# Turning the K cache with VectorE block transpositions instead of TensorE transposes in a decode step (adaLN, cached sliding-window attention, squared-ReLU MLP)

## The chip, the cores and the metric

The kernel runs on one core of a Trainium2 chip. The metric is device time of one execution in microseconds (us), lower is better. A core has TensorE (PE in the profile), VectorE (DVE), ScalarE (ACT), GpSimd (POOL) and SyncE (SP, here the engine that issues the large loads), each with its own queue that it works off in order, and 16 DMA engines that move data between HBM and the core's SBUF. Matrix products land in PSUM, eight banks of 128 partitions x 512 fp32 values. All data here is fp32.

## What is computed

One decode step for 8 sequences: a conditioning vector `c` gives six modulation vectors; then layer norm, attention over the last 2048 cached positions with 32 query heads on 8 key/value heads of width 128, layer norm again, and an MLP with squared ReLU.

```python
mod = (_silu(c) @ w_mod).reshape(c.shape[0], 6, 1, -1)          # (8,512) @ (512,3072)
h = _layernorm(x) * (1 + ca) + sa
# attention: Hq=32, Hkv=8, Dh=128, Sk=8192, W=2048
q = (h @ wq)                                                    # (512,4096)
k, v = k_cache[:, :, Sk - W:, :], v_cache[:, :, Sk - W:, :]     # each used by 4 query heads
p = softmax(q @ k.T * Dh ** -0.5)
x = x + ga * ((p @ v) @ wo)                                     # (4096,512)
h = _layernorm(x) * (1 + cb) + sb
x = x + gb * (relu(h @ w1 + b1) ** 2 @ w2 + b2)                 # F = 1792
```

The windows of K and V are 67.1 MB each; the weights are some 30.5 MB more. Every byte is used once.

## The kernel before, in words

**Loads.** All large loads go out from SyncE's queue, in the order of the list `loads` (lines 143 to 153), into fixed slots in SBUF: two "big" slots of 4.19 MB (32 KB per partition) and five "small" ones of 2.10 MB. `pump()` issues the next load of the list as soon as a slot of its size is free, and `done()` frees a slot where its last reader has been issued; the load then waits on the chip for that reader. The list is strict: a load that waits for its slot holds up all that stand behind it. It begins with K block 0, four modulation weights, four q weights, K block 1, V block 0, K block 2; after that K and V blocks and pieces of `wo` alternate, and the last entries are V block 31, the biases, `tail` (the last part of `wo` and half of `w1`, a big slot), the rest of `w1` (a small slot) and `w2` (a big slot).

**K and V blocks.** A K block `q` (16 of them) holds four sequences of one key/value head: partition `4p + u` holds 64 consecutive positions of sequence `u`. Block `2 hk` has sequences 0 to 3 of head `hk`, block `2 hk + 1` sequences 4 to 7. A V block `n` (32 of them) holds two sequences of one head.

**Turning K.** A score product needs K with the 128 values of a key along the partitions. `transposes(q, g, e)` (line 223) does an eighth of a block: eight PE transposes of 128x128 (line 232) into PSUM, two banks of them in the pool `ps_kt`, and two copies of 128x512 out of PSUM into the tile `kT` (line 234), one by ACT and one by DVE. The tile pool `ktp` has three `kT` buffers, each for one `(q, g)`. After the last eighth of a block, `done(("K", q))` frees its slot (line 237).

**Scores.** `scores(q, g)` (line 346) makes four products, one per sequence `u`, of 32 columns of q times 512 keys. The 32 columns are a sliding window over a tile of zeros with the four query heads in the middle (`qwin`, line 186, filled by `window`, line 343, out of `qall`), so the four heads land on other rows for each `(g, c)` and all eight `(g, c)` of one head add up in one PSUM bank `s_ps`: 128 rows (sequence `u`, key group `g`, half `c`, query head) by 512 keys.

**Softmax.** `soft_a` copies the scores to SBUF (ACT) and takes row maxima (DVE). `soft_b` turns the maxima into a row with PE and shares the maximum among the rows of one query head. `soft_c` brings it back to a column, and ACT's exponential writes `pr`, every fourth element, so that DVE can double it (line 410). `soft_d` turns `pr` with eight PE transposes (line 426) and DVE multiplies them out of PSUM with a mask `mine` (line 429), which keeps for each partition the half of the sequences that it holds.

**Weighted sum.** `weighted(n, h)` (line 441) multiplies the turned probabilities with a V block in two halves; behind the second half DVE adds up the diagonal blocks into `o_sb` (lines 464 and 466). `gather` and `project_o` bring the head's result through `wo` into `wo_ps`.

**Order.** The schedule is written out by hand: the loop at line 502 has 37 steps `s`; each of the first 32 turns half a K block (four calls of `transposes`) and makes two groups of scores, and V runs five steps behind (`PV_LAG`). Each engine works in the order of the calls. Ahead of the loop, the four parts of K block 0 (`EARLY`, line 263) are turned between the modulation products, and the fourth in step 0. `turn_q(0)` and `turn_q(1)` (line 328) turn the two halves of q, the second in step 1. Step 2 is the first that works on K block 1. Behind the loop come the output projection, the second layer norm and the MLP, with a few products that only keep PE busy (`spin`).

Of the kernel before, what the change touches and what calls it, by code (L numbers as in the profile page):

```python
# [20 lines left out]
def tile_adaln_cached_attention_mlp(  # L21
# [34 lines left out]
    ktp = ctx.enter_context(tc.tile_pool(name="ktp", bufs=3))  # L56
    ps_kt = ctx.enter_context(tc.tile_pool(name="ps_kt", bufs=2, space=bass.MemoryType.PSUM))
# [140 lines left out]
    u4 = consts.tile([P, 4], F32, name="u4")  # L198
    nc.vector.tensor_reduce(u4, ident.rearrange("p (u x) -> p u x", u=4), axis=AX.X, op=ALU.add)
    for c in range(2):  # L200
        nc.vector.tensor_scalar(bq[:, 4 * c : 4 * c + 4], u4, uq[:, c : c + 1], None, op0=ALU.mult)
# [11 lines left out]

    mine = consts.tile([P, 2, REP], F32, name="mine")
    odd = ident.rearrange("p (r u) -> p u r", u=2)
    for u in range(2):
        nc.vector.tensor_reduce(mine[:, u, 0:1], odd[:, u, :], axis=AX.X, op=ALU.add)
        for t in range(1, REP):
            nc.vector.tensor_copy(mine[:, u, t : t + 1], mine[:, u, 0:1])

    KTS = {}

    def transposes(q, g, e):

        k = slot(("K", q), DH)
        if e == 0:
            KTS[q, g] = ktp.tile([P, 4, 16, 32], F32, name="kT")
        t = KTS[q, g]
        for a in range(2):
            p = ps_kt.tile([P, 4, P], F32, name="kt_ps")  # L230
            for i in range(4):
                nc.tensor.transpose(p[:, i, :], k[:, 32 * e + 16 * a + 4 * g + i, :], ident)  # L232
            i = 8 * e + 4 * a
            (nc.vector.tensor_copy if a else nc.scalar.copy)(  # L234
                t[:, :, i : i + 4, :], p.rearrange("p i (r u) -> p u i r", u=4)
            )
        if g == 3 and e == 1:
            done(("K", q))
# [24 lines left out]
    EARLY = [(0, g) for g in range(4)]  # L263
# [23 lines left out]
    for kc in range(NQ):  # L287
        if kc < 3:
            transposes(0, kc, 0)
            transposes(0, kc, 1)  # L290
        wv = slot(("mod", kc), 6 * D)[:, 0].rearrange("p (m q n) -> p m q n", m=6, q=NQ)
        for pm, m0, m1 in zip(pms, (0, 4), (4, 6)):
            for q in range(NQ):
                nc.tensor.matmul(  # L294
                    pm[32 * q : 32 * q + 32, : (m1 - m0) * P].rearrange("p (m n) -> p m n", n=P),
                    cT[:, kc, :],
                    wv[:, m0:m1, q, :],
                    start=(kc == 0),
                    stop=(kc == NQ - 1),
                )  # L300
        done(("mod", kc))
# [26 lines left out]
    def turn_q(r):  # L328
        qs = work.tile([P, 512], F32, name="qs", tag="a", bufs=1)
        nc.scalar.copy(qs, pqs[r])  # L330
        pT_ = ps_m.tile([P, 512], F32, name="m_ps", tag="m_ps")
        for t in range(REP):
            nc.tensor.transpose(pT_[:, t * P : (t + 1) * P], qs[:, t * P : (t + 1) * P], ident)  # L333
        nc.vector.tensor_copy(  # L334
            qall[:, 4 * r : 4 * r + 4].rearrange("p g b t -> p t g b"),
            pT_.rearrange("p (t g b) -> p t g b", t=REP, g=4)[:, :, :, :B],
        )
# [4 lines left out]
    P_, PT_, RZ_, RZP_, OS_, O_, MX_, SS_ = {}, {}, {}, {}, {}, {}, {}, {}  # L342
    def window(hk):
        nc.vector.tensor_copy(qwin[hk % 2][:, :, 28:32], qall[:, hk])  # L344

    def scores(q, g):

        hk, c = divmod(q, 2)
        if c == 0 and g == 0:
            s_ps[0] = ps_1.tile([P, 512], F32, name="s_ps")  # L350
            if hk == 0:
                window(0)
        if c == 1 and g == 0 and hk + 1 < HKV:
            window(hk + 1)
        o = 28 - 4 * (2 * g + c)
        kT = KTS.pop((q, g))
        for u in range(4):
            nc.tensor.matmul(  # L358
                s_ps[0][32 * u : 32 * u + 32, :],
                qwin[hk % 2][:, 4 * c + u, o : o + 32],  # L360
                kT[:, u].rearrange("p i r -> p (i r)"),
                start=(c == 0 and g == 0),
                stop=(c == 1 and g == 3),
            )
# [8 lines left out]
    def soft_b(hk):  # L373
        pm = ps_m.tile([P, 512], F32, name="m_ps", tag="m_ps")
# [5 lines left out]
            pm[0:1, :P].rearrange("p (u g r) -> p u r g", u=4, g=4),  # L380
# [3 lines left out]
        nc.vector.tensor_scalar(  # L384
            mrow.rearrange("p u (g r) -> p u g r", g=4),
            m1.rearrange("p (u r) -> p u r", u=4)[:, :, None, :].to_broadcast([1, 4, 4, 8]),
            -SCALE,
            None,
            op0=ALU.mult,
        )  # L390
        MX_[hk] = mrow

    def soft_c(hk):
# [6 lines left out]
        pr = work.tile([P, 8, H, 2], F32, name="pr", bufs=1)  # L400
        z = work.tile([P, 1], F32, name="z")
        nc.scalar.activation(  # L402
            pr.rearrange("p i (r e) u -> p e i r u", e=2)[:, :, :, :, 0],
            SS_.pop(hk).rearrange("p (e i r) -> p e i r", e=2, i=8),
            AF.Exp,
            bias=nm,
            scale=SCALE,
            accum_out=z,
        )
        nc.vector.tensor_copy(pr[:, :, :, 1], pr[:, :, :, 0])  # L410
        zs = work.tile([P, B], F32, name="zs")
        nc.vector.tensor_scalar(zs, bq, z, None, op0=ALU.mult)  # L412
        P_[hk], RZP_[hk] = pr, zs
# [5 lines left out]
    def soft_d(hk):  # L419

        pr = P_.pop(hk)
        PT_[hk] = work.tile([P, 2, 4 * C, 4, 2 * REP], F32, name="pT", bufs=1)
        for a in range(2):
            pp = ps_m.tile([P, 512], F32, name="m_ps", tag="m_ps")
            for i in range(4):
                nc.tensor.transpose(  # L426
                    pp[:, i * P : (i + 1) * P], pr[:, 4 * a + i].rearrange("p r u -> p (r u)"), ident
                )
            nc.vector.tensor_mul(  # L429
                PT_[hk][:, a].rearrange("p x i r -> p i x r"),  # L430
                pp.rearrange("p (i x r) -> p i x r", i=4, r=2 * REP),
                mine.rearrange("p u t -> p (u t)")[:, None, None, :].to_broadcast([P, 4, 4 * C, 2 * REP]),
            )
# [7 lines left out]
    def weighted(n, h):  # L441
# [6 lines left out]
        for g in range(4):  # L448
            j = 16 * h + 4 * g
            nc.tensor.matmul(  # L450
                o[32 * g : 32 * g + 32].rearrange("p j d -> p (j d)"),
                PT_[hk][:, h, 4 * c + g].rearrange("p i r -> p (i r)"),
                v[:, j : j + 4, :].rearrange("p j d -> p (j d)"),
                start=(h == 0),
                stop=(h == 1),
            )
# [44 lines left out]

    for s in range(N + PV_LAG + 1):
# [27 lines left out]
        if s == 0:  # L530
            transposes(0, 3, 0)
            transposes(0, 3, 1)
# [13 lines left out]
    spin_ps = ps_kt.tile([P, 4, P], F32, name="kt_ps")  # L546
# [117 lines left out]
```

## Time and profile before

| what | value |
|---|---|
| median of 3 runs | 397.34 us (397.11 to 398.51) |
| the profiled execution | 397.39 us |
| its span, first to last instruction | 395.6 us |
| DMA traffic in the span | 165.22 MB, mean 418 GB/s |
| ACT busy | 97.5 us |
| mean granted PE clock | 0.974 |

The span is what the trace covers; the profiled execution's own time is the span and a little before and after it. Busy time of an engine counts computing instructions only. In the lists of groups a row is: line, engine, operation, output<-input by the program's names, shapes, count, then busy time in us and mean ns of one, then the idle time of the engine just before these instructions and what ended it.

### The profile page before, as it was taken

Reading aid. Unit: us, or ns where it says so; the run is one execution under the profiler, and the core shown is the slowest. Engines: PE = TensorE matmul, PEld = TensorE weight load, DVE = VectorE, ACT = ScalarE, POOL = GpSimd, SP = SyncE. Lnnn points to the kernel's source line nnn. Section 1 sums busy time; section 2 is a strip of 40 time slices with the busy share of each in tenths; the row PEclk is TensorE's granted clock in tenths of the full one; section 3 lists DMA queues with packets and bytes.
Section 4 is the critical chain, followed back from the end, with each engine's and each line's share of the span. In section 5 each row is a group of like instructions: output and inputs, shape, how many; then the busy total and the mean of one; then the engine's idle time right before and its main releaser. Section 6 shows DMA issues by size and latency. Waiting matters only on the chain.

```text
span 395.6 us, 5981 instructions
## 1 busy us (share of the span) xinstructions
PE 330.5 (84%) x2550; PEld 162.4 (41%) x2550; DVE 178.2 (45%) x416; ACT 97.5 (25%) x169; POOL 2.4 (1%) x12
## 2 busy tenths in 40 slices
PE   0683489979998697999889988998859998997696
PEld 0440035554454353444444544444534454432133
DVE  6121023454456353655464556454524455455531
ACT  2220022342232122322332222222211241222010
POOL 2000000000000000000000000000000000000000
PEclk9996889999999998999999999999999999999999
DMA  8999999999999999999999999999999999999993
GB/s 335 410 430 427 441 418 442 417 419 446 404 435 442 414 432 422 441 417 451 403 449 409 444 416 434 434 419 421 437 419 447 417 437 413 431 431 421 422 424 136
DMA packets 10363, 165.22 MB, mean 418 GB/s; under 512 B 1112, under 2 KB 1376, under 8 KB 1632
## 3 DMA queue, kind: packets, MB, share of 16 engines
q1 hardware_dynamic: 10192, 164.71, 97.9%
q8 instruction: 20, 0.33, 0.3%
q10 hardware_dynamic: 144, 0.13, 0.1%
q14 instruction: 7, 0.06, 0.0%
HBM read 164.77 MB, written 0.07 MB: 417 GB/s over the span
## 4 chain that ended last, share of the span: by engine, by line
DMA 46%; PE 42%; DVE 7%; ACT 4%; issue 1%; ACTq 0%; DVEq 0%
DMA big<-in_A_k_cache_dram 31%; PE kt_ps L232 20%; PE s_ps L358 9%; PE o_ps L450 7%; DMA small<-in_A_wq_dram 6%; DMA big<-in_B_w_dram 5%; DMA small<-in_A_v_cache_dram 4%; ACT pr L402 2%; DVE o_sb L466 2%; DVE kT L234 2%; PE m_ps L294 1%; ACT kT L234 1%; DVE pT L429 1%; PE m_ps L319 1%; DVE pr L410 1%
## 5 line engine op out<-in xcount | busy, mean ns | idle before, releaser
L232 PE MATMUL kt_ps<-ident,big 128*128 128x128 f32 x1024 | 145.5, 285 | 22.6 <-DMA big<-in_A_k_cache_dram 18.3
L232 PEld LDWEIGHTS kt_ps<-ident,big 128*128 128x128 f32 x1024 | 112.8, 144 | 111.9 <-ACT kT L234 68.1
L234 DVE COPY kT<-kt_ps 128x512 f32<-128x512 f32 x128 | 88.2, 689 | 121.5 <-PE kt_ps L232 121.5
L234 ACT COPY kT<-kt_ps 128x512 f32<-128x512 f32 x128 | 75.0, 586 | 209.4 <-PE kt_ps L232 208.6
L358 PE MATMUL s_ps<-kT,qwin 128*32 128x512 f32 x512 | 69.2, 614 | 0.8 <-DVE qwin L344 0.8
L450 PE MATMUL o_ps<-small,pT 128*32 128x512 f32 x512 | 67.1, 602 | 1.9 <-DMA small<-in_A_v_cache_dram 1.9
L466 DVE SCALAR_TENSOR_TENSOR o_sb<-o_ps,diag,o_sb 128x128 f32<-128x128 f32 x96 | 33.7, 351 | 3.4
L319 PE MATMUL m_ps<-small,h1T 128*32 128x512 f32 x64 | 11.5, 857 | 11.5 <-DMA small<-in_A_wq_dram 11.5
L450 PEld LDWEIGHTS o_ps<-small,pT 128*32 128x32 f32 x512 | 11.7, 108 | 22.7 <-issue 22.7
L464 DVE TENSOR_SCALAR o_sb<-o_ps,diag 128x128 f32<-128x128 f32 x32 | 11.2, 350 | 16.3 <-PE o_ps L450 15.6
L358 PEld LDWEIGHTS s_ps<-kT,qwin 128*32 128x32 f32 x512 | 10.3, 109 | 12.8 <-issue 11.1
L402 ACT ACTIVATE pr<-ss,nm 128x512 f32<-128x512 f32 x8 | 9.9, 1244 | 11.8 <-DVE nm L399 11.7
L334 DVE COPY qall<-m_ps 128x128 f32<-128x128 f32 x2 | 0.8, 390 | 23.0 <-PE m_ps L333 23.0
L435 PE MATMUL m_ps<-zs,tsel 128*128 128x8 f32 x16 | 3.1, 266 | 8.7 <-DVE pT L429 8.7
L319 PEld LDWEIGHTS m_ps<-small,h1T 128*32 128x32 f32 x64 | 2.1, 134 | 19.8 <-DMA small<-in_A_wq_dram 10.6
L429 DVE TENSOR_TENSOR pT<-m_ps,mine 128x512 f32<-128x512 f32 x16 | 10.2, 680 | 0.0
L474 PE MATMUL m_ps<-o_sb,pick 128*128 128x512 f32 x16 | 8.4, 606 | 1.8 <-DVE o_sb L466 1.6
L426 PEld LDWEIGHTS m_ps<-ident,pr 128*128 128x128 f32 x64 | 6.9, 141 | 7.0 <-issue 7.0
L426 PE MATMUL m_ps<-ident,pr 128*128 128x128 f32 x64 | 8.7, 278 | 1.1 <-DVE zs L412 1.1
L370 DVE TENSOR_REDUCE mx<-ss 128x1 f32<-128x512 f32 x8 | 5.5, 688 | 8.6 <-ACT ss L368 8.6
L410 DVE COPY pr<-pr 128x512 f32<-128x512 f32 x8 | 3.4, 430 | 12.3 <-ACT pr L402 12.3
L294 PE MATMUL m_ps<-small,cT 128*32 128x512 f32 (+1 forms) x64 | 6.6, 531 | 1.3 <-DMA small<-in_w_mod_dram 1.3
(123 smaller groups left out, 105.4 us busy)
## 6 DMA issues: line engine op xcount, KB each, us to landing
big<-in_A_k_cache_dram SPq DMA_DIRECT2D x16, 4096.0 KB, 21.9
small<-in_A_v_cache_dram SPq DMA_DIRECT2D x32, 2048.0 KB, 23.2
small<-in_A_wq_dram SPq DMA_DIRECT2D x4, 2048.0 KB, 21.8
small<-in_w_mod_dram SPq DMA_DIRECT2D x4, 1536.0 KB, 17.4
small<-in_A_wo_dram SPq DMA_DIRECT2D x3, 2048.0 KB, 19.9
big<-in_A_wo_dram SPq DMA_DIRECT2D x2, 1024.0 KB, 17.8
big<-in_B_w_dram SPq DMA_DIRECT2D x1, 2048.0 KB, 23.4
big<-in_B_w_dram SPq DMA_DIRECT2D x1, 1792.0 KB, 22.0
```

The lines of the kernel that those rows point to most:

```text
L232: nc.tensor.transpose(p[:, i, :], k[:, 32 * e + 16 * a + 4 * g + i, :], ident)
L234: (nc.vector.tensor_copy if a else nc.scalar.copy)(t[:, :, i : i + 4, :], p.rearrange("p i (r u) -> p u i r", u=4))
L294: nc.tensor.matmul(pm[32 * q : 32 * q + 32, : (m1 - m0) * P].rearrange("p (m n) -> p m n", n=P), cT[:, kc, :], wv[:, m0:m1, q, :], start=( ...
L319: nc.tensor.matmul(pqs[r][32 * g : 32 * g + 32, :], hT[:, kc, :], w[:, 4 * r + g, :], start=(kc == 0), stop=(kc == NQ - 1),)
L358: nc.tensor.matmul(s_ps[0][32 * u : 32 * u + 32, :], qwin[hk % 2][:, 4 * c + u, o : o + 32], kT[:, u].rearrange("p i r -> p (i r)"), start ...
L402: nc.scalar.activation(pr.rearrange("p i (r e) u -> p e i r u", e=2)[:, :, :, :, 0], SS_.pop(hk).rearrange("p (e i r) -> p e i r", e=2, i= ...
L426: nc.tensor.transpose(pp[:, i * P : (i + 1) * P], pr[:, 4 * a + i].rearrange("p r u -> p (r u)"), ident)
L429: nc.vector.tensor_mul(PT_[hk][:, a].rearrange("p x i r -> p i x r"), pp.rearrange("p (i x r) -> p i x r", i=4, r=2 * REP), mine.rearrange ...
L450: nc.tensor.matmul(o[32 * g : 32 * g + 32].rearrange("p j d -> p (j d)"), PT_[hk][:, h, 4 * c + g].rearrange("p i r -> p (i r)"), v[:, j : ...
L464: nc.vector.tensor_scalar(d, o[:, 0, :], diag[:, 0:1], None, op0=ALU.mult)
L466: nc.vector.scalar_tensor_tensor(d, o[:, j, :], diag[:, j : j + 1], d, op0=ALU.mult, op1=ALU.add)
L474: nc.tensor.matmul(pp, pick.rearrange("p t u -> p (t u)"), o.rearrange("p c d -> p (c d)"), start=True, stop=True)
```

## The change

K is turned by DVE's transposition, which turns each 32x32 square of a tile by itself, directly from SBUF to SBUF. One call of `transposes(q, j, e)` is now a single DVE instruction on 32 of a block's 64 positions and on 32 of the 128 values. A square of 32 partitions holds eight groups `p` of four sequences `u`; behind the transposition partition `32 i + x` holds value `32 j + x` of the keys that lay on partitions `32 i` to `32 i + 31`. So a `kT` tile holds one quarter `j` of the values for all keys of the block, and on its partitions lie four different key groups `i`. The score product must take quarter `j` of q on each of the four partition groups, and put the result of group `i` on rows of its own: `qst` holds q in such pieces with zeros between them. They are made per head by a product with `sel` that repeats a quarter `j` of q on all four partition groups (`window`), out of `qbd`, which holds q block by block between zeros; four ACT and four DVE copies put them in place.

The score rows then stand in another order (sequence, key group, half, query head); `soft_b` multiplies the copied scores with a permutation matrix `perm`, and the exponential reads the result out of PSUM and writes `pr` contiguously. `pr2` takes the place of the doubling and of the mask: DVE and ACT write one half each, multiplied with 0 or 1. One DVE transposition of 128x1024 takes the place of eight PE transposes and two masked copies in `soft_d`.

The pool `ps_kt` is gone (its two banks go to the products of `window` and `soft_b`), there are two `kT` buffers in place of three, and only two of the four parts of K block 0 are turned ahead of the loop; the other two are turned in step 1 by the loop itself.

```diff
-    ktp = ctx.enter_context(tc.tile_pool(name="ktp", bufs=3))
-    ps_kt = ctx.enter_context(tc.tile_pool(name="ps_kt", bufs=2, space=bass.MemoryType.PSUM))
+    ktp = ctx.enter_context(tc.tile_pool(name="ktp", bufs=2))
...
-    qall = consts.tile([P, HKV, B, REP], F32, name="qall")
-    qwin = [consts.tile([P, B, 60], F32, name=f"qwin{i}") for i in range(2)]
-    for t in qwin:
+    qbd = consts.tile([P, HKV, 4, B * REP], F32, name="qbd")
+    qst = [consts.tile([P, B, 4, 4, 2, REP], F32, name=f"qst{i}") for i in range(2)]
+    for t in [qbd, *qst]:
         nc.gpsimd.memset(t, 0.0)
...
+    perm = consts.tile([P, P], F32, name="perm")
+    nc.vector.tensor_copy(
+        perm.rearrange("r (i u w) -> r i u w", i=4, u=4), ident.rearrange("r (u i w) -> r i u w", i=4, u=4)
+    )
...
-    def transposes(q, g, e):
+    def transposes(q, j, e):
         k = slot(("K", q), DH)
         if e == 0:
-            KTS[q, g] = ktp.tile([P, 4, 16, 32], F32, name="kT")
-        t = KTS[q, g]
-        for a in range(2):
-            p = ps_kt.tile([P, 4, P], F32, name="kt_ps")
-            for i in range(4):
-                nc.tensor.transpose(p[:, i, :], k[:, 32 * e + 16 * a + 4 * g + i, :], ident)
-            i = 8 * e + 4 * a
-            (nc.vector.tensor_copy if a else nc.scalar.copy)(
-                t[:, :, i : i + 4, :], p.rearrange("p i (r u) -> p u i r", u=4)
-            )
-        if g == 3 and e == 1:
+            KTS[q, j] = ktp.tile([P, 4, 64, 8], F32, name="kT")
+        rows = slice(32 * e, 32 * e + 32)
+        nc.vector.transpose(
+            KTS[q, j][:, :, rows].rearrange("q u r p -> q r p u"),
+            k[:, rows, 32 * j : 32 * j + 32].rearrange("q r (p u) -> q r p u", u=4),
+        )
+        if j == 3 and e == 1:
             done(("K", q))
...
-    EARLY = [(0, g) for g in range(4)]
+    EARLY = [(0, 0), (0, 1)]
...
-        if kc < 3:
+        if kc < 2:
             transposes(0, kc, 0)
             transposes(0, kc, 1)
...
-        nc.vector.tensor_copy(
-            qall[:, 4 * r : 4 * r + 4].rearrange("p g b t -> p t g b"),
-            pT_.rearrange("p (t g b) -> p t g b", t=REP, g=4)[:, :, :, :B],
-        )
+        for j in range(4):
+            b = slice(32 * j, 32 * j + 32)
+            nc.vector.tensor_copy(
+                qbd[b, 4 * r : 4 * r + 4, j].rearrange("p g (b t) -> p t g b", t=REP),
+                pT_[b].rearrange("p (t g b) -> p t g b", t=REP, g=4)[:, :, :, :B],
+            )
...
     def window(hk):
-        nc.vector.tensor_copy(qwin[hk % 2][:, :, 28:32], qall[:, hk])
+        pq = ps_1.tile([P, 512], F32, name="q_ps")
+        nc.tensor.matmul(pq[:, :P], sel, qbd[:, hk].rearrange("p j x -> p (j x)"), start=True, stop=True)
+        pv = pq[:, :P].rearrange("p (j c u t) -> p c u j t", j=4, c=2, u=4)
+        for i in range(4):
+            b = slice(32 * i, 32 * i + 32)
+            for c in range(2):
+                (nc.vector.tensor_copy if c else nc.scalar.copy)(
+                    qst[hk % 2][b, 4 * c : 4 * c + 4, :, i, c], pv[b, c]
+                )
...
-                qwin[hk % 2][:, 4 * c + u, o : o + 32],
-                kT[:, u].rearrange("p i r -> p (i r)"),
+                qst[hk % 2][:, 4 * c + u, j].rearrange("p i c t -> p (i c t)"),
+                kT[:, u].rearrange("q r p -> q (r p)"),
...
     def soft_b(hk):
+        sp = ps_1.tile([P, 512], F32, name="p_ps")
+        nc.tensor.matmul(sp, perm, SS_.pop(hk), start=True, stop=True)
+        SS_[hk] = sp
...
     def soft_c(hk):
...
-        nc.vector.tensor_copy(pr[:, :, :, 1], pr[:, :, :, 0])
+        X_[hk] = work.tile([P, 32, 8, 2, 2], F32, name="pr2", bufs=1)
+        for c in range(2):
+            o, i = X_[hk][:, :, :, :, c], pr.rearrange("p e j x -> p j x e")
+            if c:
+                nc.scalar.mul(o, i, uq[:, c : c + 1])
+            else:
+                nc.vector.tensor_scalar(o, i, uq[:, c : c + 1], None, op0=ALU.mult)
...
     def soft_d(hk):
-        for a in range(2):
-            pp = ps_m.tile([P, 512], F32, name="m_ps", tag="m_ps")
-            for i in range(4):
-                nc.tensor.transpose(
-                    pp[:, i * P : (i + 1) * P], pr[:, 4 * a + i].rearrange("p r u -> p (r u)"), ident
-                )
-            nc.vector.tensor_mul(
...
+        PT_[hk] = work.tile([P, 4, 32, 2 * REP], F32, name="pT", bufs=1)
+        nc.vector.transpose(
+            PT_[hk].rearrange("p u j r -> p j u r"),
+            X_.pop(hk).rearrange("p j (u r) e c -> p j u (r e c)", u=4),
+        )
...
-        if s == 0:
-            transposes(0, 3, 0)
-            transposes(0, 3, 1)
```

More of the change, by code (lines that the diff above doesn't have):

```diff
@@ L383, in soft_b @@
         )
[L384 to L389, printed above, removed]
-        )
+        nc.vector.tensor_scalar(mrow, m1[:, None, :].to_broadcast([1, 4, 32]), -SCALE, None, op0=ALU.mult)
         MX_[hk] = mrow
```

49 lines of the change are left out of this document (14 added, 35 removed).

## The prediction, on record before the change was run

> **What bounds the kernel now.** I read the busy line and the table of stretches first, then the chain that ended last and SyncE's waits, then the groups by shape for prices. In a row of the stretches the columns are the stretch, its length, busy time of PE, PE's weight loads, DVE, ACT and GpSimd, the granted clock, the DMA engines' share, and GB/s.
>
> ```profile
> span 395.6 us, 5981 instructions
> PE 330.5 (84%) x2550; PEld 162.4 (41%) x2550; DVE 178.2 (45%) x416; ACT 97.5 (25%) x169; POOL 2.4 (1%) x12
> 0.00:5.00 5.00, 0.00 (x0) 0.00 (x0) 3.47 (x23) 1.59 (x2) 2.43 (x12) 1.00 0.67 249
> 5.00:10.00 5.00, 0.84 (x4) 0.76 (x4) 3.28 (x16) 0.78 (x3) 0.00 (x0) 1.00 0.99 426
> 10.00:50.00 40.00, 23.59 (x166) 10.14 (x170) 6.20 (x13) 5.31 (x10) 0.00 (x0) 0.86 1.01 429
> 50.00:90.00 40.00, 34.94 (x258) 19.03 (x254) 15.26 (x30) 13.92 (x23) 0.00 (x0) 0.97 0.99 422
> 250.00:290.00 40.00, 37.20 (x285) 18.62 (x283) 21.11 (x45) 11.53 (x20) 0.00 (x0) 1.00 1.01 430
> 10.00:380.00 370.00, 317.78 (x2392) 155.98 (x2392) 168.69 (x370) 94.82 (x164) 0.00 (x0) 0.97 1.01 427
> ```
>
> PE is the busiest engine at 84%, but the DMA engines are full: share 1.01 and 427 GB/s from 10 to 380 us, and hardly different in stretches where PE works 23.6 or 37.2 us of 40. By the shapes of the inputs 164.7 MB must come in (K and V 67.1 each, the weights 30.5); nothing on the engines can shorten that.
>
> ```profile
> 0.73 12.61 DMA big<-in_A_k_cache_dram
> 211.35 20.18 DMA big<-in_A_k_cache_dram
> 250.34 20.18 DMA big<-in_A_k_cache_dram
> 369.82 20.87 DMA big<-in_B_w_dram
> 390.73 1.76 PE m_ps L617 x48
> SPq L108 <- PE kt_ps L232: 250.9, 30, 27.3
> ```
>
> The chain (start, length, what) shows the cycle: a K block is asked for, lands 20.2 us later, PE turns it, and the next K load into that slot goes out; 211.35 to 250.34 is 39.0 us. That cycle loads two K blocks of 4.19 MB and four V blocks of 2.10 MB, 16.8 MB, and 16.8 MB at 430 GB/s is 39.0 us. So the slot cycle and the transfer are equal, and SyncE waits for PE (250.9 us) only because the queue already holds enough. The end is the last weight load, landed at 390.7, and 4.9 us of work behind it. I call four steps of the loop, one `hk` with its two K blocks, a head: 39.0 us now. The sum below is made against the profiled execution, 397.39 us, which is 1.79 us over its span and within 0.05 us of the median 397.34.
>
> **What goes away, and what it is worth.**
>
> ```profile
> L232 PE MATMUL kt_ps<-ident,big 128*128 128x128 f32 x1024 | 145.5, 285 | 22.6 <-DMA big<-in_A_k_cache_dram 18.3 <-ACT kT L234 3.4
> L234 DVE COPY kT<-kt_ps 128x512 f32<-128x512 f32 x128 | 88.2, 689 | 121.5 <-PE kt_ps L232 121.5
> L234 ACT COPY kT<-kt_ps 128x512 f32<-128x512 f32 x128 | 75.0, 586 | 209.4 <-PE kt_ps L232 208.6 <-DVE kT L234 0.8
> L429 DVE TENSOR_TENSOR pT<-m_ps,mine 128x512 f32<-128x512 f32 x16 | 10.2, 680 | 0.0
> L410 DVE COPY pr<-pr 128x512 f32<-128x512 f32 x8 | 3.4, 430 | 12.3 <-ACT pr L402 12.3
> ```
>
> PE loses 145.5 us, ACT 75.0 and DVE 88.2 + 10.2 + 3.4 = 101.8. Since the transfers set the time, these are worth 0 as long as the transfers go on without a gap. What is late next is DVE, which must now turn all of K.
>
> **The price of one K transposition.** There are 16 x 4 x 2 = 128 of them, each 128 x 1024 elements SBUF to SBUF. Read: runs of 32. Write: `q r p u` into `kT[q, u, r, p]`, innermost `u` 512 elements (2 KB) apart, so no element lands beside the one before it. No row shows this; these are the nearest.
>
> ```profile
> L478 DVE STREAM_TRANSPOSE tr<-m_ps 128x512 f32<-128x512 f32 x8 | 5.7, 717 | 3.3 <-PE m_ps L474 3.3
> L243 DVE STREAM_TRANSPOSE rc<-m_ps 128x448 f32<-128x448 f32 x1 | 0.7, 650 | 1.3 <-PE m_ps L598 1.3
> L399 DVE COPY nm<-m_ps 128x1 f32<-128x1 f32 x8 | 1.3, 157 | 4.1 <-PE m_ps L395 4.1
> L554 DVE COPY at_i<-wo_ps 128x256 f32<-128x256 f32 x1 | 0.4, 425 | 1.2 <-PE wo_ps L490 1.2
> L334 DVE COPY qall<-m_ps 128x128 f32<-128x128 f32 x2 | 0.8, 390 | 23.0 <-PE m_ps L333 23.0
> L402 ACT ACTIVATE pr<-ss,nm 128x512 f32<-128x512 f32 x8 | 9.9, 1244 | 11.8 <-DVE nm L399 11.7
> L580 ACT ACTIVATE sq<-x,nmean 128x128 f32<-128x128 f32 x1 | 0.4, 401 | 1.9 <-DVE nmean L574 1.9
> ```
>
> Lower end: transpositions with contiguous writes grow by (717 - 650)/64 = 1.05 ns per element, so 1024 cost 717 + 512 x 1.05 = 1.25 us. Upper end and middle come from scattered writes. DVE copies out of PSUM with contiguous writes grow by (425 - 157)/255 = 1.05 ns, so 128 elements should take 157 + 134 = 291; L334 has 128 elements whose writes step by four elements (16 bytes), and took 390: 0.78 ns more per element. ACT's exponential writes 512 elements 16 bytes apart in 1244; its contiguous neighbour L580 took 401 for 128, and at 0.84 ns per element (586 for 512 against 373 for 256 in L555) 512 would be 724:
>
> ```profile
> L555 ACT COPY at_i<-wo_ps 128x256 f32<-128x256 f32 x1 | 0.4, 373 | 17.6 <-DVE at_i L554 17.6
> ```
>
> 1.02 ns more per element. So a transposition costs 1.25 + 1024 x 0.78 = 2.05 us by DVE's row and 2.29 by ACT's. I take 2.05: same engine, same kind of write. 128 x 2.05 is 262 us in place of the 88 us of copies.
>
> [...]
>
> **DVE's work in one head, with waits.**
>
> ```profile
> L466 DVE SCALAR_TENSOR_TENSOR o_sb<-o_ps,diag,o_sb 128x128 f32<-128x128 f32 x96 | 33.7, 351 | 3.4
> L464 DVE TENSOR_SCALAR o_sb<-o_ps,diag 128x128 f32<-128x128 f32 x32 | 11.2, 350 | 16.3 <-PE o_ps L450 15.6
> L370 DVE TENSOR_REDUCE mx<-ss 128x1 f32<-128x512 f32 x8 | 5.5, 688 | 8.6 <-ACT ss L368 8.6
> L378 DVE TENSOR_REDUCE m<-m_ps 1x32 f32<-1x128 f32 x8 | 2.2, 277 | 1.0 <-PE m_ps L375 0.5
> L384 DVE TENSOR_SCALAR mrow<-m 1x128 f32<-1x128 f32 x8 | 1.7, 216 | 0.3
> L412 DVE TENSOR_SCALAR zs<-bq,z 128x8 f32<-128x8 f32 x8 | 1.8, 224 | 0.0
> L439 DVE RECIPROCAL rz<-m_ps 128x8 f32<-128x8 f32 x8 | 1.6, 196 | 0.0
> L479 DVE TENSOR_TENSOR oT<-tr,rz 128x32 f32<-128x32 f32 x8 | 1.7, 216 | 0.4
> ```
>
> Kept: (33.7 + 11.2)/8 = 5.6 for `o_sb`; the small ones (5.5 + 2.2 + 1.7 + 1.3 + 1.8 + 1.6 + 5.7 + 1.7)/8 = 2.7; together 8.3. New: turning the probabilities, 1024 elements with writes in runs of eight, 1.25; DVE's half of `pr2`, 0.43 (L410) to 0.83 (with 0.78 ns more per element for its scattered reads), I take 0.7; four window copies of 64 elements from PSUM at 157 + 67 = 0.22 each, 0.9; together 2.9. Waiting in order: DVE stood before L410 for 12.3, L370 8.6, L399 4.1, L478 3.3, that is 3.5 us a head; the same chain (score copy, maximum, exponential) stays, so I keep 3.5, between 0 and double. Transpositions: 16 x 2.05 = 32.8. A head on DVE is 32.8 + 8.3 + 2.9 + 3.5 = 47.5 us, against 39.0 for the transfers. At 1.25 us it is 34.7, under them; in one head the two meet at (39.0 - 14.7)/16 = 1.52 us. Behind a transposition that waits for its K block, or for one of now two `kT` buffers, stand DVE's `o_sb` sums and maxima, and behind those PE's products, which need `o_ps` banks; the `kT` wait itself is covered, as PE's score product for the older buffer is 1 us and queued one transposition earlier (uncovered it costs 1 us for each of 64).
>
> Hidden: PE's two products per head more (selection, permutation; some 2 us in 145.5/8 = 18 us of freed PE time per head), ACT's four copies and one multiplication (75 us freed), GpSimd's larger zeroing (needed at 53.6 us; GpSimd does nothing after the first 5), the `perm` copy (DVE works 6.2 us from 10 to 50). Without that cover each would cost a few us once, or PE's 2 us a head.
>
> **The start.**
>
> ```profile
> 57.88 0.53 SPq L108 DMA_DIRECT2D big<-in_A_k_cache_dram  x1
> 53.60 0.38 DVE L334 COPY qall<-m_ps 128x128 f32<-128x128 f32 x1 [22.38 <-PE m_ps L333]
> L358 PE MATMUL s_ps<-kT,qwin 128*32 128x512 f32 x512 | 69.2, 614 | 0.8 <-DVE qwin L344 0.8
> ```
>
> K block 2 is asked for at 57.88, when block 0 has been turned. Ahead of it stand 25.2 MB (two K, the modulation and q weights, one V). By the stretches 1.2 + 2.1 + 17.2 = 20.5 MB are in by 50 us, so at 422 GB/s the queue runs dry at 61.2. The first load shows 1.4 us from issue (0.73) to first bytes (1.2 MB by 5.0 at 429). So a load issued after 59.8 leaves a gap. With only two `kT` buffers the second half of block 0 can't be turned early: DVE starts at 53.6 with four copies of L334's form (1.6), then selection product and four window copies (1.6), scores (69.2 over 64 groups, 1.1), the second half of q (product 0.7, copies 1.6): 60.2. Four transpositions make it 68.4 (65.2 at 1.25 us). Block 2 goes out then.
>
> **The sum.** From 68.4, 30 steps or 7.5 heads remain: 7.5 x 47.5 = 356, less 5.6 (no `o_sb` in the first four) and 4.5 (no softmax in half a head): 346, so the last K block is turned at 414.4. Only then can the last V block and behind it the last weights go out: 2.10 + 3.93 + 1.84 + 3.67 = 11.5 MB by their shapes, 1.4 + 26.9 us; then 4.9 as now: span 447.6, time 449.4 us.
>
> **Rivals.**
> (a) DVE stays under the transfers: scattered writes cost a transposition nothing, 1.25 us. For it: L478 itself rearranges, at full rate; but its writes are contiguous. Then only the gap at the start counts: 65.2 + 1.4 - 61.2 = 5.4, time 402.8. [...]
> (b) In between. The sum above falls by 124 x (2.05 - T) and meets (a)'s time at T = 1.67 us, later than in one head because the first heads are lighter and the queue is short at the end; from there to 1.8 us: 403 to 418.
> (c) Not slower: as (a), but block 2 is asked for before 59.8. That needs block 0 turned about 6 us sooner than I worked out: the copies and the second half of q would have to lie outside the path of its four transpositions. The decisive point is 59.8; then no gap, 397.4.
> (d) Faster: no gap at the start, and the transfers speed up when the engines use SBUF otherwise. For it, one 40 us stretch shows 430 against the mean 427; against it, the stretches stay at 422 to 430 whatever PE does. At 430 throughout, 164.7/0.427 = 385.7 us of transfer become 383.0: 394.7. [...]
> (e) PE's clock falls to half, since PE is busy half the time.
>
> ```profile
> 150.00:155.00 5.00, 2.92 (x16) 1.77 (x16) 0.69 (x1) 0.59 (x1) 0.00 (x0) 0.66 0.99 423
> L450 PE MATMUL o_ps<-small,pT 128*32 128x512 f32 x512 | 67.1, 602 | 1.9 <-DMA small<-in_A_v_cache_dram 1.9
> ```
>
> The clock was 0.66 in the stretch with a PE pause. PE's head is (69.2 + 67.1)/8 = 17 us plus about 3, 40 at half clock against 39.0 for the transfers: 7.5 more than (a), 410, with DVE at 1.25.
>
> **How the numbers follow.** Forecast (DVE-bound, 1.8 us or more) 0.52; (a) 0.22, (b) 0.10, (c) 0.08, (d) 0.05, (e) 0.03. The forecast's own range: 1.8 us gives 418, 2.05 without any wait 423, with double waits 476, 2.29 us 449.4 + 124 x 0.24 = 479; so 418 to 479. To hold 8 in 10 the whole range takes in (a), (b) and (e): 401 to 479. About 0.5% is what a measurement here can tell from no change. Faster by that 0.05, within it 0.08, slower 0.87.
>
> **What would show it.** The row of the K transposition: about 2.05 us, x128. DVE busy about 365 us (178.2 - 101.8 + 262 + 8 x 2.9 + 3 at the start), PE under 205 (330.5 - 145.5 + 8 x 2). DMA share well under 1 from 70 us on, with SyncE's K loads waiting for DVE; a dip at 61 to 70 us. The prediction is wrong if that row is under 1.5 us, or if DMA stays at 427 GB/s through the middle.

## The result, and the profile after

The change makes the kernel slower: 420.4 us (median of four, 418.51 to 422.56) against 397.23 (median of four; the 397.34 above is of the first three), a ratio of 1.058 (95% interval 1.052 to 1.063). The forecast was 449.4 in a range of 401 to 479: the right direction and inside the range, but the step is 23 us where 52 were forecast. The profiled execution took 418.51 us, 1.8 over its span.

The busy line and the table of stretches of the changed kernel (columns as before: stretch, length, PE, weight loads, DVE, ACT, GpSimd, clock, DMA share, GB/s):

```profile
span 416.7 us, 3775 instructions
PE 247.8 (59%) x1494; PEld 60.2 (14%) x1494; DVE 328.4 (79%) x430; ACT 33.4 (8%) x81; POOL 4.2 (1%) x13
10.00:50.00 40.00, 17.19 (x122) 4.46 (x126) 9.36 (x12) 2.57 (x6) 0.00 (x0) 0.91 1.02 431
60.00:70.00 10.00, 4.92 (x21) 0.75 (x18) 9.97 (x8) 0.00 (x0) 0.00 (x0) 0.67 0.27 106
130.00:170.00 40.00, 24.35 (x148) 5.62 (x148) 37.22 (x45) 2.87 (x8) 0.00 (x0) 0.87 1.01 431
250.00:290.00 40.00, 24.42 (x144) 5.63 (x148) 36.70 (x46) 3.02 (x8) 0.00 (x0) 0.83 0.96 400
67.80:374.80 307.00, 186.35 (x1034) 41.05 (x1034) 282.18 (x320) 22.47 (x57) 0.00 (x0) 0.79 0.98 412
```

DVE is now the full engine: 282 of the 307 us of the loop (67.8 to 374.8, from the request for K block 2 to the last K block turned), some 37 of 40 in the two later stretches shown. The transfers show the hole that was forecast at 61 to 70 us (106 GB/s) and fall to 400 GB/s in a stretch like 250 to 290; over the loop their share is 0.98, so they are still nearly full. Where the queue has enough, they run at 431 while DVE works 37.2 of 40 us (130 to 170): no slowing of the transfers by DVE's traffic shows there.

The chain that ended last, as shares of the span, and three of its pieces (start, length, what):

```profile
DVE 55%; PE 15%; ACT 3%; issue 2%; ACTq 0%; DVEq 0%
371.19 3.62 DVE kT L225 x2
385.29 8.88 PE o_ps L444 x64
410.38 3.24 PE m_ps L607 x112
```

Before, 46% of it was DMA. Now the chain can be followed back to 102.6 us, three quarters of the span, and no transfer is in that part. From groups by shape and the time line:

```profile
L225 DVE STREAM_TRANSPOSE kT<-big 128x1024 f32<-128x1024 f32 x128 | 238.4, 1937 | 0.7 <-DMA big<-in_A_k_cache_dram 0.6
L424 DVE STREAM_TRANSPOSE pT<-pr 128x1024 f32<-128x1024 f32 x8 | 9.9, 1232 | 0.0
60.50 12.62 DVE L225 STREAM_TRANSPOSE kT<-big 128x1024 f32<-128x1024 f32 x7
67.76 0.54 SPq L107 DMA_DIRECT2D big<-in_A_k_cache_dram  x1
```

The two transpositions turn the same number of elements; the one with scattered writes takes 1937 ns, the one with writes in runs of eight 1232. Seven K transpositions running take 12.62 us, 1.80 each, where seven records of 1.937 would be 13.56: records of neighbours on DVE overlap, here by about 0.15 us at each of the six joins, so the mean of one is more than its share of the queue.

Three parts make up the difference. In the kernel before, the last K block is turned at 351.1, by the row below; after the change at 374.8 (371.19 + 3.62, above):

```profile
350.12 1.02 PE kt_ps L232 x8
```

| part | before | after | difference |
|---|---|---|---|
| start to the request for K block 2 | 57.9 | 67.8 | +9.9 |
| from there to the last K block turned | 293.2 | 307.0 | +13.8 |
| from there to the end of the span | 44.5 | 41.9 | -2.6 |
| span | 395.6 | 416.7 | +21.1 |

### The profile page after: what moved, and what is told of

Same layout as the page of the kernel before. It is cut to its first block, busy times and chain, and to the rows that moved or that the text cites. A ratio compares the mean times of both kernels' runs of the same rounds, so it can differ in the third digit from the quotient of the medians.

```text
span 416.7 us, 3775 instructions
## 1 busy us (share of the span) xinstructions
PE 247.8 (59%) x1494; PEld 60.2 (14%) x1494; DVE 328.4 (79%) x430; ACT 33.4 (8%) x81; POOL 4.2 (1%) x13
## 4 chain that ended last, share of the span: by engine, by line
DVE 55%; PE 15%; ACT 3%; issue 2%; ACTq 0%; DVEq 0%
DVE kT L225 40%; DVE o_sb L460 6%; PE o_ps L444 5%; PE s_ps L361 4%; PE p_ps L378 2%; DVE pT L424 2%; DVE o_sb L458 1%; ACT pr L402 1%; PE q_ps L541 1%; DVE qst L346 1%; DVE mx L373 1%; DVE tr L472 1%; ACT qst L346 1%; DVE pr L412 1%; PE m_ps L588 1%
## 5 line engine op out<-in xcount | busy, mean ns | idle before, releaser
L225 DVE STREAM_TRANSPOSE kT<-big 128x1024 f32<-128x1024 f32 x128 | 238.4, 1937 | 0.7 <-DMA big<-in_A_k_cache_dram 0.6
L361 PE MATMUL s_ps<-kT,qst 128*32 128x512 f32 x512 | 91.5, 794 | 125.4 <-DVE kT L225 102.6
L444 PE MATMUL o_ps<-small,pT 128*32 128x512 f32 x512 | 86.6, 753 | 0.0
L361 PEld LDWEIGHTS s_ps<-kT,qst 128*32 128x32 f32 x512 | 11.4, 120 | 181.8 <-DVE kT L225 145.8
L444 PEld LDWEIGHTS o_ps<-small,pT 128*32 128x32 f32 x512 | 19.1, 130 | 50.1 <-issue 45.2
L346 ACT COPY qst<-q_ps 32x64 f32<-32x64 f32 x32 | 6.5, 203 | 125.3 <-PE q_ps L341 94.0
L378 PE MATMUL p_ps<-ss,perm 128*128 128x512 f32 x16 | 13.1, 913 | 0.0
L346 DVE COPY qst<-q_ps 32x64 f32<-32x64 f32 x32 | 6.9, 215 | 7.4 <-ACT qst L346 7.4
L424 DVE STREAM_TRANSPOSE pT<-pr 128x1024 f32<-128x1024 f32 x8 | 9.9, 1232 | 0.0
L410 ACT ACTIVATE pr<-pr,uq 128x512 f32<-128x512 f32 x8 | 6.8, 850 | 0.3
```

Source lines behind the costliest of these rows:

```text
L225: nc.vector.transpose(KTS[q, j][:, :, rows].rearrange("q u r p -> q r p u"), k[:, rows, 32 * j : 32 * j + 32].rearrange("q r (p u) -> q r ...
L346: (nc.vector.tensor_copy if c else nc.scalar.copy)(qst[hk % 2][b, 4 * c : 4 * c + 4, :, i, c], pv[b, c])
L361: nc.tensor.matmul(s_ps[0][32 * u : 32 * u + 32, :], qst[hk % 2][:, 4 * c + u, j].rearrange("p i c t -> p (i c t)"), kT[:, u].rearrange("q ...
L378: nc.tensor.matmul(sp, perm, SS_.pop(hk), start=True, stop=True)
L424: nc.vector.transpose(PT_[hk].rearrange("p u j r -> p j u r"), X_.pop(hk).rearrange("p j (u r) e c -> p j u (r e c)", u=4),)
L444: nc.tensor.matmul(o[32 * g : 32 * g + 32].rearrange("p j d -> p (j d)"), PT_[hk][:, c, j : j + 4].rearrange("p i r -> p (i r)"), v[:, j : ...
```

## Experiments

Three theories were on record. D: DVE's queue sets the loop's pace, because the scattered writes make a transposition dear. C: PE's lower granted clock (0.815 on the mean, before 0.974) makes the products late. G: the hole in the transfers at the start shifts all that follows.

**1. Writes side by side.** The tile takes the transposed values in the order in which they come, and PE reads every fourth.

```diff
-            KTS[q, j] = ktp.tile([P, 4, 64, 8], F32, name="kT")
+            KTS[q, j] = ktp.tile([P, 64, 8, 4], F32, name="kT")
...
-            KTS[q, j][:, :, rows].rearrange("q u r p -> q r p u"),
+            KTS[q, j][:, rows],
...
-                kT[:, u].rearrange("q r p -> q (r p)"),
+                kT[:, :, :, u].rearrange("q r p -> q (r p)"),
```

> K transposition writes contiguously (kT laid out as positions, groups, sequences); the score product reads every fourth element. Nothing else changes. Theory D (DVE's scattered writes hold the loop's pace): the transposition falls from 1.94 to about 1.25 us, a head from 41.9 to the transfers' 39 to 41 us, the time from 420 to 402 to 406 us; the gap of the transfers at 61 to 67 us stays. Theory C (PE's lower granted clock makes the products late): DVE gets faster but the time stays above 414. If reading every fourth element costs PE much more than now (794 ns per record), PE becomes the bound and the time says nothing on D alone.

Measured: 402.47 us (400.97 to 403.19), 1.010 of the kernel before (1.005 to 1.015). Groups by shape, then two stretches:

```profile
L225 DVE STREAM_TRANSPOSE kT<-big 128x1024 f32<-128x1024 f32 x128 | 151.5, 1219 | 45.0 <-DMA big<-in_A_k_cache_dram 44.9
L361 PE MATMUL s_ps<-kT,qst 128*32 128x512 f32 x512 | 127.3, 1073 | 85.4 <-DVE kT L225 79.1
60.00:70.00 10.00, 7.62 (x38) 1.15 (x37) 9.45 (x11) 0.20 (x1) 0.00 (x0) 1.00 0.36 137
90.00:370.00 280.00, 199.03 (x1044) 40.17 (x1044) 197.24 (x326) 22.34 (x55) 0.00 (x0) 0.91 1.00 428
```

One layout gives back 18 of the 23 us. DVE now stands 45 us waiting for K blocks (0.6 before this edit), and from 90 us on the transfers are full again: transfers are 52% of the chain that ended last. That PE's score products became dearer (1073 ns for 794) cost nothing that can be seen.

**2. The order of loads.** V blocks 1 and 2 go out ahead of K block 2, so the queue does not run dry at 61 us.

```diff
+    for v in (2, 1):
+        loads.remove(("V", v))
+        loads.insert(loads.index(("V", 0)) + 1, ("V", v))
```

> Only the order of loads changes: V blocks 1 and 2 go out ahead of K block 2, so the queue has work from 61 to 71 us. Theory D: DVE has enough K at that time and stays the bound, so the dip in the transfers goes and the time stays at 420 (418 to 422). Theory G (the transfers are the bound throughout and the gap of some 8 us shifts all that follows): 412 to 414.

Measured: 419.88 us (419.12 to 421.39), no change. Stretches:

```profile
60.00:70.00 10.00, 4.93 (x24) 1.04 (x27) 9.07 (x9) 0.00 (x0) 0.00 (x0) 0.50 1.01 431
80.00:90.00 10.00, 4.55 (x20) 0.40 (x16) 9.09 (x7) 0.59 (x1) 0.00 (x0) 0.50 0.41 164
100.00:110.00 10.00, 5.40 (x30) 1.46 (x34) 10.00 (x9) 0.59 (x1) 0.00 (x0) 0.60 0.25 108
```

The time is as theory D said, but the dip did not go, as D had also expected: the hole is filled at 60 and stands at 80 and 100 us instead. The shortage was moved, not removed, so the run by itself decides nothing on theory G. What speaks against G as the main cause stands in other rows: DVE waits 0.6 us in all for K blocks in the changed kernel, and experiment 1 gives back 18 of the 23 us with the hole still there (137 GB/s).

**3. Both edits.**

> Both: contiguous writes and V blocks 1 and 2 ahead of K block 2. Theory D: with DVE under the transfers the gap is what is left of the loss, so this run is 4 to 6 us faster than contiguous writes alone, 397 to 400, level with the kernel before. Theory G alone: the same as the reordered loads alone, 412 to 414. Theory C: no better than 410.

Measured: 402.62 us (401.57 to 403.38), the same as contiguous writes alone. A miss: 397 to 400 was expected. K block 2 is asked for at 64.9 us, but lands behind the two V blocks, and the shortage comes again at 90 us. What is scarce at the start is not work for the queue but a free K slot, and loads in another order do not free one (experiment 6 does).

**4. A busier PE.** Three products that nobody reads in each of steps 2 to 33.

```diff
+        if 2 <= s < N + 2:
+            wp = ps_1.tile([P, 512], F32, name="q_ps").rearrange("p (a n) -> p a n", a=4)
+            for _ in range(3):
+                nc.tensor.matmul(wp, ident, ident[:, None, :].to_broadcast([P, 4, P]), start=True, stop=True)
```

> Adds three PE products of 128x512 that nobody reads to each of steps 2 to 33, so PE is busy enough for a higher granted clock. Theory C: the clock rises from 0.8 to over 0.95, the products come 0.2 us sooner each and the time falls by 5 us or more. Theory D: the clock rises and the time stays within 3 us of 420.

Measured: 451.49 us (451.04 to 454.7). Inconclusive as a test of the clock: it rose only from 0.815 to 0.864, and the added products came onto the chain themselves (18% of it, by line 530). It shows that PE at this clock has little room in the order of the changed kernel's queues.

**5. Block 0 turned early.** All four parts of K block 0 are turned ahead of the loop; parts 2 and 3 lie in the fifth small slot until their products are made. Writes stay scattered.

```diff
+    free["small"].remove(V_SLOTS - 1)
...
+            if q == 0 and j > 1:
+                KTS[q, j] = slots["small"][V_SLOTS - 1][:, 2048 * (j - 2) : 2048 * (j - 1)].rearrange(
+                    "q (u r p) -> q u r p", u=4, r=64
+                )
...
-    EARLY = [(0, 0), (0, 1)]
+    EARLY = [(0, j) for j in range(4)]
...
+        if (q, j) == (0, 3):
+            free["small"].append(V_SLOTS - 1)
+            pump()
```

> The changed kernel, scattered writes as they are, but all four parts of K block 0 are turned ahead of the loop; the third and fourth lie in the fifth small slot until their products are made, and that slot takes loads only afterwards. Theory D: the loop starts without the 4 x 1.8 = 7.2 us of transpositions of step 1, K block 2 goes out before 61 us, no gap; the loop itself stays bound by DVE at some 42 us a head: 411 to 414. If the start were worth nothing, 420.

Measured: 415.82 us (413.13 to 417.66): 4.6 us better, fewer than the 6 to 9 expected.

```profile
L231 DVE STREAM_TRANSPOSE kT<-big 128x1024 f32<-128x1024 f32 x124 | 231.1, 1935 | 2.6 <-DMA big<-in_A_k_cache_dram 2.5
```

K block 2 is asked for at 36.5 us in place of 67.8, and DVE comes to block 1 7 us sooner, but part is lost again later on: DVE waits 2.5 us for K blocks where it waited 0.6. The rest was not traced.

**6. Early turning and writes side by side.**

> Contiguous writes and block 0 turned early. Theory D with the late second half of block 0 as the cause of the 5 us that contiguous writes left: 397 to 398.5, level with the kernel before, no dip in the transfers at 61 us. If the 5 us come from elsewhere (PE's slower reading of every fourth element, the longer way of q): 402.

Measured: 396.28 us (395.86 to 396.8, ten runs), 0.996 of the kernel before (0.9936 to 0.9984). Stretches:

```profile
60.00:70.00 10.00, 8.74 (x42) 1.85 (x38) 7.04 (x12) 0.81 (x4) 0.00 (x0) 0.98 1.02 437
10.00:380.00 370.00, 255.48 (x1335) 51.95 (x1335) 234.80 (x392) 29.77 (x75) 0.00 (x0) 0.92 1.01 428
```

No hole, transfers full from 10 to 380 us as before the change; K block 2 is asked for at 37.6 us. So the two causes together are the whole loss: 18 us from the scattered writes, and then 6 from the late second half of block 0. Taken in the other order they are 4.6 (experiment 5) and 19.5 (from there to here): what one is worth depends on what binds. The two `kT` buffers and the longer way of q, which this kernel keeps, cost nothing that can be seen.

**7. The same DVE time without scattered writes.** Experiment 1, and behind each K transposition a DVE maximum over 592 zeros.

```diff
...
+        nc.vector.tensor_reduce(padt, padw[:, :592], axis=AX.X, op=ALU.max)
...
```

> Contiguous writes, and behind each K transposition one DVE maximum over 592 elements of a tile of zeros that nobody reads, some 0.70 us, which is what the scattered writes cost. Theory D (it is DVE's time and nothing about the writes themselves, such as a slowing of transfers or of PE): the time goes back to 417 to 422. If the scattered writes hurt in another way: clearly under 412.

Measured: 416.55 us (416.08 to 416.86). Three DVE rows of the time line and two groups:

```profile
63.44 1.23 DVE L228 STREAM_TRANSPOSE kT<-big 128x1024 f32<-128x1024 f32 x1
64.59 0.73 DVE L232 TENSOR_REDUCE padt<-padw 128x1 f32<-128x592 f32 x1
65.24 1.23 DVE L228 STREAM_TRANSPOSE kT<-big 128x1024 f32<-128x1024 f32 x1
L228 DVE STREAM_TRANSPOSE kT<-big 128x1024 f32<-128x1024 f32 x128 | 157.5, 1231 | 2.7 <-DMA big<-in_A_k_cache_dram 2.6
L365 PE MATMUL s_ps<-kT,qst 128*32 128x512 f32 x512 | 127.7, 1076 | 101.0 <-DVE kT L228 99.0
```

From one transposition to the next 1.80 us (63.44 to 65.24), as with scattered writes, and 14 of the 18 us are back, just short of the 417 to 422 expected. So at least 14 of the 18 are DVE's time, and not what the writes do to others. The granted clock here is 0.90, as in experiment 1 (0.90 to 0.93), so these 14 are not theory C's; it can account for no more than the 4 us that are left. They stay open; in this kernel `kT` is also ready 0.65 us before the padding ends, which scattered writes don't give. Neither was tested by itself.

**8. Half the padding.** 256 zeros in place of 592.

> Contiguous writes and behind each K transposition a DVE maximum over 256 elements, some 0.35 us, half of what the scattered writes cost. Theory D with a threshold at about 1.65 us per transposition: 1.14 + 0.35 = 1.5 lies under it, so 402 to 405, nearly nothing, where the whole 0.70 cost 14. If DVE's time counted in proportion: 409.

Measured: 403.48 us (401.32 to 403.98). Two rows of the time line:

```profile
62.96 1.23 DVE L228 STREAM_TRANSPOSE kT<-big 128x1024 f32<-128x1024 f32 x1
64.42 1.23 DVE L228 STREAM_TRANSPOSE kT<-big 128x1024 f32<-128x1024 f32 x1
```

At 1.46 us from one transposition to the next, DVE takes 286 us in all, and the time is 1 us over that of 1.14. So with 1.14, 1.46 and 1.80 us the times are 402.5, 403.5 and 416.6: nearly nothing for the first step and 13 us for the second, so a threshold lies between 1.46 and 1.80. How steep the time rises beyond it, three points do not show.

**9. Prices of writes and reads.** One K block is loaded, then eight each of several forms run; nothing of the reference is computed.

> Computes nothing of the reference: one K block is loaded, then eight each of DVE transpositions of 128x1024 with writes contiguous, 8 bytes apart, 16 bytes apart, in four interleaved runs 32 bytes apart, and 2 KB apart; DVE copies of 128x512 with writes contiguous, 8 and 16 bytes apart; ACT copies contiguous and 16 bytes apart; PE products of 512 columns reading contiguously, every fourth element, and runs of eight. If the price is that of leaving a 16-byte stretch with each element: 1.2 us contiguous and at 8 bytes, 1.9 at 16 bytes, 32 bytes and 2 KB alike. If it is the distance: 16 bytes well under 2 KB. PE: contiguous 0.6 us a pair at full clock, every fourth about 1.0.

The DVE and PE time lines (start, busy for eight, line; lines 79, 81, 85, 89, 93 are writes contiguous, 8 bytes apart, 16 bytes apart, interleaved runs 32 bytes apart, 2 KB apart; lines 120, 122, 126 are reads contiguous, every fourth, runs of eight; a product is two records):

```profile
13.32 9.13 DVE L79 STREAM_TRANSPOSE near<-src 128x1024 f32<-128x1024 f32 x8 [12.32 <-DMA src<-in_A_k_cache_dram]
22.38 9.09 DVE L81 STREAM_TRANSPOSE far<-src 128x1024 f32<-128x1024 f32 x8
31.39 14.64 DVE L85 STREAM_TRANSPOSE far<-src 128x1024 f32<-128x1024 f32 x8
45.86 14.68 DVE L89 STREAM_TRANSPOSE near<-src 128x1024 f32<-128x1024 f32 x8
60.37 14.15 DVE L93 STREAM_TRANSPOSE far<-src 128x1024 f32<-128x1024 f32 x8
26.10 7.03 PE L120 MATMUL flat<-src,st 128*32 128x512 f32 x16
32.97 14.56 PE L122 MATMUL step<-src,st 128*32 128x512 f32 x16
47.35 7.05 PE L126 MATMUL runs<-src,st 128*32 128x512 f32 x16
```

Not the distance counts: eight transpositions took 14.64 us with writes 16 bytes apart and 14.15 at 2 KB. Eight bytes cost nothing (9.09 against 9.13). The DVE copies of 128x512 from SBUF, contiguous (line 97) and with writes 16 bytes apart (line 104):

```profile
L97 DVE COPY near<-src 128x512 f32<-128x512 f32 x8 | 2.7, 424 | 0.0
L104 DVE COPY far<-src 128x512 f32<-128x512 f32 x8 | 3.8, 648 | 0.0
```

Per element they pay 0.44 ns more ((648 - 424)/512), less than a transposition does, and 8 bytes apart hardly anything (449 ns). ACT's copies go from 619 to 1141 ns, 1.02 ns more per element.

**10. Prices, continued.**

> Computes nothing of the reference: prices of DVE transpositions of 128x1024 with writes contiguous, in jumping pairs, 16 bytes apart and 12 bytes apart, and of PE products of 512 columns that read every element, every second, third and fourth. If two hits running on one 16-byte stretch are enough: pairs 1.14 us each, 12 bytes apart between (a third of the writes share a stretch with the one before). PE: every second element 0.44 per record as contiguous, every third between, every fourth 0.91.

Lines 79, 81, 88, 92: contiguous, jumping pairs, 16 and 12 bytes apart; PE lines 100 to 110: every element, second, third, fourth:

```profile
22.26 9.09 DVE L81 STREAM_TRANSPOSE far<-src 128x1024 f32<-128x1024 f32 x8
31.27 14.64 DVE L88 STREAM_TRANSPOSE far<-src 128x1024 f32<-128x1024 f32 x8
45.73 11.08 DVE L92 STREAM_TRANSPOSE far<-src 128x1024 f32<-128x1024 f32 x8
25.26 7.03 PE L100 MATMUL flat<-src,st 128*32 128x512 f32 x16
32.13 7.36 PE L102 MATMUL step<-src,st 128*32 128x512 f32 x16
39.33 10.97 PE L106 MATMUL step<-src,st 128*32 128x512 f32 x16
50.13 14.57 PE L110 MATMUL step<-src,st 128*32 128x512 f32 x16
```

Jumping pairs of neighbouring writes are as cheap as contiguous writes (9.09 us for eight against 9.13); single writes 12 bytes apart are dearer (11.08).

**11. Pairs, with block 0 early.** The price list suggests a layout that is cheap for both engines (9.09 us for eight on DVE, 7.36 for 16 records on PE): two sequences side by side.

```diff
-            KTS[q, j] = ktp.tile([P, 4, 64, 8], F32, name="kT")
+            KTS[q, j] = ktp.tile([P, 2, 64, 8, 2], F32, name="kT")
...
-            KTS[q, j][:, :, rows].rearrange("q u r p -> q r p u"),
-            k[:, rows, 32 * j : 32 * j + 32].rearrange("q r (p u) -> q r p u", u=4),
+            KTS[q, j][:, :, rows].rearrange("q a r p b -> q (r p) a b"),
+            k[:, rows, 32 * j : 32 * j + 32].rearrange("q r (p a b) -> q r p a b", a=2, b=2),
...
-                kT[:, u].rearrange("q r p -> q (r p)"),
+                kT[:, u // 2, :, :, u % 2].rearrange("q r p -> q (r p)"),
```

> Block 0 turned early, and kT laid out so that two sequences lie side by side: the transposition writes two neighbours, jumps, writes two neighbours; PE reads every second element. If a 16-byte stretch must only be hit twice running for the full rate, the transposition takes 1.2 us as with contiguous writes and PE keeps its price (0.6 us per record at full clock, against 1.07 with every fourth element). The transfers bind either way: 395.5 to 397, level with contiguous writes and early turning. If pairs aren't enough for DVE, 1.9 us and 413 to 417.

Measured: 396.46 us (395.9 to 396.8, twelve runs), 0.9976 of the kernel before (0.9963 to 0.9988).

```profile
L231 DVE STREAM_TRANSPOSE kT<-big 128x1024 f32<-128x1024 f32 x124 | 147.0, 1220 | 40.0 <-DMA big<-in_A_k_cache_dram 39.9
L367 PE MATMUL s_ps<-kT,qst 128*32 128x512 f32 x496 | 84.3, 756 | 102.7 <-DVE kT L231 98.4
```

Both prices are low now, and the time is that of experiment 6: the transfers bind. PE's granted clock was 0.82 to 0.87 in these twelve runs, about as low as in the changed kernel, and the time is still that of the kernel before: the low clock alone cost nothing here, where the transfers bind.

**12. Pairs alone.**

> Only the pairs, without early turning. Theory D: 401 to 403.5, as contiguous writes, since the late second half of block 0 stays; PE's cheaper reading is worth nothing while transfers bind. If PE's reading was part of the 5 us that contiguous writes left: 398 to 400.

Measured: 401.73 us (400.69 to 402.55), as contiguous writes alone. PE's slower reading was no part of what they left.

## Why the prediction was right and wrong

- **The bound.** Right. The transfers were full before, so 145 us of PE work less bought under 1 us even where nothing else was lost (396.3 and 396.5 in experiments 6 and 11), and with scattered writes DVE took the transfers' place.
- **The start.** Right to the microsecond: 68.4 us for the request of K block 2, measured 67.8; the transpositions began at 60.5 where 60.2 was worked out. Turning block 0 early is worth 5 us while DVE binds (experiment 5) and 6 where the transfers bind (experiments 1 and 6).
- **The price of one transposition.** The direction was right: scattered writes make DVE slower, by about as much at 16 bytes as at 2 KB (1.83 and 1.77 us against 1.14, experiment 9). The size was a little too high: 2.05 us against 1.94 as a record, 0.69 ns more per element and not 0.78. That it came so near is in part luck: row L334 is a copy out of PSUM, and copies out of SBUF pay 0.44 ns for the same writes (experiment 9). Rival (a)'s 1.25 us is near what contiguous writes cost (1.22 us as a record in experiment 1, 1.14 each in experiment 9) and not what these do.
- **The step that failed** is "DVE's work in one head", 47.5 us. It added record lengths as if each instruction had the queue to itself. Neighbours overlap, and a head took 40.9 us on the mean (307/7.5). From 67.8 to 374.8 us the sum said 346: 246 of transpositions, 75 of other work and 25 of waits. Measured are 307: 224 under transpositions (below), 58 other work (282 - 224) and 25 of waits. The two sums of records were 39 us too long. Of these about 21 are the overlap: the records of this stretch add up to 232 + 70 = 303 us, and DVE was busy for 282. Another 14 are the price (120 times 2.05 in place of 1.94), and 5 are other work that was put too high.

The transpositions alone in that stretch (columns: stretch, length, busy, clock, DMA share, GB/s):

```profile
67.80:374.80 307.00, 223.86 (x120) 0.79 0.98 412
```

- **The waits.** Right in their sum, 25 us, and in this by luck. The forecast kept the waits for scores, maximum and exponential. Of these only some 10 us are left in the loop (7.8 below, and 2.3 for the maximum); others came in their place, for ACT's window copies and for the maxima that PE turns into a row (what waited, for what: us, times, longest):

```profile
DVE pr L412 <- ACT pr L402: 7.8, 7, 2.2
DVE qst L346 <- ACT qst L346: 5.6, 21, 0.3
DVE m L384 <- PE m_ps L381: 5.0, 5, 2.8
```

- **The end.** Forecast as the remaining loads, 33.2 us from the last K block turned; measured 41.9. V block 31 goes out 3.7 us after the last K block is turned, since it waits for V products that free a small slot; the transfers end at about 408, and the last V products and the chain of the projection and the MLP reach the last product only at 410.38. From the last weight to the end it is 8.6 us and not 4.9. This took back 9 of the 39 us, so the forecast's error would have been larger without it. The request for V block 31, and the stretch in which the transfers end:

```profile
378.53 0.53 SPq L107 DMA_DIRECT2D small<-in_A_v_cache_dram  x1
408.00:410.00 2.00, 2.00 (x6) 0.76 (x4) 0.77 (x3) 0.00 (x0) 0.00 (x0) 1.00 0.10 37
```

- **The signs.** The transposition's row (1.94 us, x128), the dip at 61 to 70 us and SyncE's K loads waiting for DVE (149.0 us) came as forecast. DVE busy is 328.4 us and not 365, by the overlap and the price. The transfers' share was to lie well under 1 from 70 us on and was 0.98 in the loop: DVE was the slower of the two by little, 40.9 us a head against 39.0. PE is 247.8 us and not under 205: its score products grew from 614 to 794 ns and its V products from 602 to 753 as the granted clock fell from 0.974 to 0.815, and the forecast had kept the old lengths.
- **Rival (a)** turned out nearly to the figure once the writes were made contiguous: 402.8 forecast, 402.5 measured; the threshold was put at 1.67 us, and experiments 7 and 8 show it between 1.46 and 1.80. Rival (c)'s condition, block 2 asked for in time, gives 396.3 with contiguous writes, where 397.4 was forecast. Rival (d) does not show: in that run the transfers move 428 GB/s from 10 to 380 us, 427 before. Rival (e) happened in part: PE's clock fell to 0.815. It isn't the main cause: experiment 7 leaves it 4 us at most, and in experiment 11 a clock as low cost nothing.

## What to carry to other kernels

When transfers are full, taking work off the busiest engine gains next to nothing (here under 1 us for 145 us less on PE), and the engine that takes it over must stay under the transfers' pace with all it has to do: here 0.3 us more per transposition cost 1 us in all below that threshold, and as much again, which passed it, 13. Before accepting a layout that scatters an engine's writes, look whether two neighbours can be kept together: here that alone is worth 18 us and more (420.4 to 401.73, experiment 12). To add up an engine's queue, take the distance from one instruction to the next out of the time line (here 1.80 us), not the mean length of a record (1.94).

## What the runs showed of the hardware

In series of eight DVE transpositions of 128x1024 fp32, one took 1.14 us with writes contiguous, 8 bytes apart or in jumping pairs, 1.39 with single writes 12 bytes apart, 1.83 at 16 bytes and in interleaved runs 32 bytes apart, and 1.77 at 2 KB (experiments 9 and 10). So with single writes the price rose between 8 and 16 bytes and was no higher at 2 KB, and with pairs it did not rise. Why that is so was not shown. Unexpected was that PE pays too when it reads its moving operand in single elements that lie apart: 7.03 us for 16 records contiguous, 7.36 with every second element, 10.97 with every third and 14.57 with every fourth, while runs of eight with gaps cost nothing (7.05).
